# Loading w_in for the first two tiles in pieces of 384, 512 and 480 columns, each summed in a PSUM bank of its own

## The chip, the cores and the metric

The kernel runs on one core of a Trainium2 chip. A core has a matrix engine (TensorE, PE in the profile), a vector engine (VectorE, DVE), an activation engine (ScalarE, ACT), a general one (GpSimd, POOL) and a queue engine (SyncE, SP); 16 DMA engines move data between the chip's main memory and the core's SBUF. TensorE multiplies out of SBUF into PSUM, which has eight banks of 512 float32 columns over 128 partitions. The metric is the device time of one execution in microseconds; the median of the runs of a kernel is compared.

## What is computed

x is 2048 rows of 512 columns. Two blocks work on it and a gate mixes them. Block A is linear attention with 32 heads of 16 and learned softmax features. Block B, the one this change touches, is a gated MLP with spatial mixing: x is multiplied by w_in (512 by 1376), a GELU follows, the right half is normalised over its columns and mixed over the rows with w_sp, and the product of both halves goes through w_out.

```
def _B_ref(x, w_in, w_sp, b_sp, w_out):
    B, S, D = x.shape
    F = w_in.shape[-1]
    Fh = F // 2
    z = _gelu(jnp.einsum('bsd,df->bsf', x, w_in))
    z1 = z[..., :Fh].copy()
    z2 = _layernorm(z[..., Fh:], axis=-1)
    g = jnp.einsum('ts,bsf->btf', w_sp, z2) + b_sp[None, :, None]
    return jnp.einsum('bsf,fd->bsd', z1 * g, w_out)
...
g = _sigmoid((x * gate_w).sum(-1, keepdims=True))
a = _A_ref(x, A_wqkv, A_w_phi, A_wo)
b = _B_ref(x, B_w_in, B_w_sp, B_b_sp, B_w_out)
return g * a + (1 - g) * b
```

## The kernel before

The 2048 rows are 16 tiles t of 128. All input is bf16 and stays in SBUF. The order of instructions on each engine is written out by hand: what the program lists first for an engine runs first on it, and semaphores are put in where one engine's instruction reads or overwrites what another one, or a DMA, has written.

The work runs in three stages. In the first, about a quarter of the time, every tile's rows are multiplied with w_in into PSUM (`z_piece`), passed through GELU into the buffer `zz` on ACT (`z_gelu`, `z_post`) and their column statistics are taken on DVE; products for block A are threaded between. In the second, 32 half tiles of w_sp times zz (`gg_half`) run among block A's key features; in the third the rest of these run among block A's queries and the output products (`out_part`).

The inner dimension of 512 is four slices of 128 (dt). `xT` holds x transposed, slice by slice, as the stationary operand; `w_in` is the moving operand, with one column more than the reference's 1376: column F holds gate_w, so the gate's product falls out of the same matmuls. It is written by `gate_column` (L208), a small matmul that turns gate_w's four rows into a column, and a cast on DVE (L212).

The change is in the first microseconds:

- x for tiles 0 and 1 is loaded as rows into `xn` (L108 on SP's queue, L109 on ACT's), transposed on TensorE (`x_transpose`, L193) and copied to `xT` by DVE for tile 0 and by ACT for tile 1 (`x_copy`, L200), in three steps over the slices. The xT of all later tiles comes by transposing DMAs on SP (L123 for tiles 2 and 3, L129 for the rest).
- w_in is loaded with seven DMAs (L112, L122), called A to E here. A is columns 0 to 256 and B is 256 to 512, both with slices 0 and 1 on SP's queue and slices 2 and 3 on ACT's. C and D are columns 512 to 1024, slices 0 and 1 and then 2 and 3, both on SP. E is columns 1024 to 1376 of all slices, on SP. The fifth transfer of a queue is held until the first one has landed, the sixth until the second, and so on.
- ACT's queue then loads gate_w (`gw`, L120), and ACT loads its GELU table (L121).
- Until the first data are there, TensorE runs matmuls on constants (`spin`, L187), whose result nobody reads.
- Tiles 0 and 1 then go through w_in together, slice by slice: columns 0 to 256, 256 to 512 and 512 to 1024 of both, with ACT's gelu of tile 0 and `gate_column` behind the second piece; then the last piece (353 columns with the gate's) of tile 0, its gelu, gate and statistics (`z_post`), and the same of tile 1, whose gelu over all 1376 columns is one instruction. Every later tile takes three pieces of 512, 512 and 353 columns.
- A tile's sums lie in three banks, 0 to 2 for even tiles and 3 to 5 for odd ones (`zbank`, L67); columns n0 to n1 lie at n0 to n1 of these 1536 columns.

Of the kernel before, what the change touches and what calls it, by code (L numbers as in the profile page):

```python
# [7 lines left out]
AF = mybir.ActivationFunctionType  # L8
# [6 lines left out]
P = 128  # L15
# [4 lines left out]
F = 1376  # L20
# [3 lines left out]
NDT = D // P  # L24
CH = 512
# [14 lines left out]
def kernel(  # L40
# [14 lines left out]
    nc = tc.nc  # L55
# [11 lines left out]
    def zbank(t):  # L67
        b = 3 * (t % 2)
        return ps[:, b:b + 3, :].rearrange("p b n -> p (b n)")

    xT = pers.tile([P, NDT, S], BF16, name="xT")
    w_in = pers.tile([P, NDT, F + 1], BF16, name="w_in")
# [6 lines left out]
    zz = pers.tile([P, NT, F], BF16, name="zz")  # L79
# [15 lines left out]
    gth = st[:, 1, :]  # L95
# [7 lines left out]
        out=ident[:], in_=ident[:], pattern=[[-1, P]],  # L103
# [3 lines left out]
    w_in_v = B_w_in.rearrange("(dt p) f -> p dt f", p=P)  # L107
# [3 lines left out]
    def load_w_in(eng, d0, d1, n0, n1):  # L111
        eng.dma_start(out=w_in[:, d0:d1, n0:n1], in_=w_in_v[:, d0:d1, n0:n1])  # L112

    HC = CH // 2
    for n0 in (0, HC):
        load_w_in(nc.sync, 0, 2, n0, n0 + HC)
        load_w_in(nc.scalar, 2, 4, n0, n0 + HC)
    for d0 in (0, 2):
        load_w_in(nc.sync, d0, d0 + 2, CH, 2 * CH)
    nc.scalar.dma_start(out=gw[:], in_=gate_w.rearrange("(dt p) -> dt p", p=P))  # L120
    nc.scalar.activation(out=st[:, 9, 0:1], in_=ones[:, 0:1], func=AF.Gelu_apprx_tanh)  # L121
    nc.sync.dma_start(out=w_in[:, :, 2 * CH:F], in_=w_in_v[:, :, 2 * CH:F])  # L122
    nc.sync.dma_start_transpose(out=xT[:, :, 2 * P:CH], in_=x2[2 * P:CH, :])  # L123
    nc.sync.dma_start(
        out=wv[:, :, :],
        in_=A_wqkv[:, 2 * D:3 * D].rearrange("(dt p) n -> p dt n", p=P),
    )
    for q in range(1, NCH):
        nc.sync.dma_start_transpose(  # L129
            out=xT[:, :, q * CH:(q + 1) * CH], in_=x2[q * CH:(q + 1) * CH, :]  # L130
        )
        if q == 1:
            nc.sync.dma_start(
                out=wphiW[:, :, :],
                in_=A_w_phi.rearrange("(g h) e f -> (h e) g f", g=NDT),
# [3 lines left out]
        out=bcolb[:, :, :], in_=B_b_sp.rearrange("(t p) -> t p", p=P)  # L139
# [7 lines left out]
    for t in range(WSLOTS):  # L147
        load_wsp(t)
    nc.sync.dma_start(
        out=w_out[:, 0:NFT - 1, :],  # L150
        in_=B_w_out[0:(NFT - 1) * P, :].rearrange("(ft p) n -> p ft n", p=P),
# [4 lines left out]
        out=w_out[0:last_m, NFT - 1, :], in_=B_w_out[(NFT - 1) * P:FH, :]  # L156
    )
    nc.sync.dma_start(
        out=wo[:, :, :], in_=A_wo.rearrange("(g p) n -> p g n", p=P)
# [4 lines left out]
        out=mask16[:], in_=mask16[:], pattern=[[-16, 8]],  # L164
# [3 lines left out]
        out=mask16[:], in_=mask16[:], pattern=[[16, 8]],  # L168
# [8 lines left out]
    def z_piece(t, n0, n1, d0=0, d1=NDT):  # L177
        zb = zbank(t)
        for dt in range(d0, d1):
            nc.tensor.matmul(  # L180
                zb[:, n0:n1], lhsT=xT[:, dt, t * P:(t + 1) * P], rhs=w_in[:, dt, n0:n1],
                start=(dt == 0), stop=(dt == NDT - 1),
            )

    Z_PIECES = [(0, CH), (CH, 2 * CH), (2 * CH, F + 1)]

    def spin(n):  # L187
        for _ in range(n):
            nc.tensor.matmul(
                ps[:, 5, 0:P], lhsT=ones, rhs=ones, start=True, stop=True  # L190
            )
# [16 lines left out]
    def gate_column():  # L208
        nc.tensor.matmul(  # L209
            ps[:, 6, 0:NDT], lhsT=gw[:], rhs=ident[0:NDT, 0:NDT], start=True, stop=True  # L210
        )
        nc.vector.tensor_copy(out=w_in[:, :, F], in_=ps[:, 6, 0:NDT])  # L212

    def z_gelu(t, n0, n1):
        nc.scalar.activation(  # L215
            out=zz[:, t, n0:n1], in_=zbank(t)[:, n0:n1], func=AF.Gelu_apprx_tanh
        )

    def z_post(t, done=0):
        zb = zbank(t)  # L220
        z_gelu(t, done, F)
        nc.scalar.activation(out=gth[:, t:t + 1], in_=zb[:, F:F + 1], func=AF.Tanh, scale=0.5)
        for h in range(2):
            nc.vector.bn_stats(  # L224
                out=stats[:, t, h, :], in_=zz[:, t, FH + h * HF:FH + (h + 1) * HF]
            )
        nc.vector.bn_aggr(out=mv[:, t, :], in_=stats[:, t, :, :].rearrange("p h s -> p (h s)"))
# [63 lines left out]
    def build_wphi():  # L291
        nc.vector.tensor_tensor(
            out=wphi[:].rearrange("p g (h f) -> p g h f", h=8),
            in0=wphiW[:, :, None, :].to_broadcast([P, NDT, 8, DH]),
            in1=mask16[:, None, :, None].to_broadcast([P, NDT, 8, DH]),
            op=ALU.mult,
        )
# [178 lines left out]
        x_copy(0, d0, d1)  # L476
        x_copy(1, d0, d1)
    spin(4)
    for n0, n1 in ((0, HC), (HC, CH), Z_PIECES[1]):
        for dt in range(NDT):  # L480
            z_piece(0, n0, n1, dt, dt + 1)
            z_piece(1, n0, n1, dt, dt + 1)
        if n1 == CH:
            z_gelu(0, 0, CH)
            gate_column()
    z_gelu(0, *Z_PIECES[1])
    z_piece(0, *Z_PIECES[2])
    z_post(0, done=2 * CH)
    z_piece(1, *Z_PIECES[2])
    z_post(1)  # L490
    build_wphi()
    for t in range(2, NT):
        for n0, n1 in Z_PIECES:
            z_piece(t, n0, n1)
        z_post(t)
        if t >= VLAG:
            v_proj(t - VLAG)
        if 5 <= t < 13:
            fold(t - 5)
        if t in (3, 7, 11):  # L500
            ln_batch(t - 3, t + 1)
        if t == 14:
            ln_batch(12, 15)
        if t == 7:
            nc.vector.tensor_copy(out=bcol[:], in_=bcolb[:, 0, :])
        if t >= 5:
            z1_gate(t - 5)
# [81 lines left out]
```

## Time and profile before

| | us |
|---|---|
| median of 3 runs | 208.22 |
| lowest, highest | 207.81, 208.29 |
| the profiled execution, whole | 208.12 |
| its span, from the first to the last instruction | 206.4 |

| DMA queue | packets | MB |
|---|---|---|
| q1, what SP issues | 87360 | 23.87 |
| q10, what ACT issues | 3000 | 2.39 |

Times inside the profile count from the start of the span. PE, DVE, ACT and POOL are the engines above; PEld is TensorE's loading of the stationary operand, which runs beside its matmuls; SPq and ACTq are the queue instructions that issue a DMA. A matmul's shown duration includes the pipeline's end, so back-to-back matmuls overlap in it: the distance of their starts is what one costs. The granted clock of TensorE was 1.000 over the span. The page's chain that ended last gives PE 96%, DMA 2%. In it L405 (w_sp times zz) holds 36%, L180 (x times w_in) 18%, and the DMA of w_in 2%.

Two shares of the DMA view are of use for the first microseconds: the mean busy share of the 16 DMA engines and the GB/s that they moved. From 2.0 to 9.0 they moved 1.87 MB, 267 GB/s in the mean, of which q10 carried 0.39 MB. DMA issues that matter there, with KB each and the median time from issue to landing: w_in on SP, two of 256 KB (4.5 us), two of 128 KB (3.6), one of 352 KB (4.9); w_in on ACT, two of 128 KB (4.0); xn, 128 KB on each queue (2.5 on SP, 2.7 on ACT). These KB are of 1024 bytes.

### The profile page before, as it was taken

The numbers are of one execution on the slowest core, as the hardware profiler recorded it, in microseconds if no ns is written. First come the engines' busy times: TensorE is split into PE (matmuls) and PEld (weight loads), VectorE is DVE, ScalarE is ACT, GpSimd is POOL, SyncE is SP. The second block draws the span as 40 slices with busy tenths as digits, with TensorE's granted clock in tenths as the row PEclk, the third lists the DMA queues.
The fourth block names the chain that finished last, engine by engine and source line by source line (L and its number), as shares of the span: only waits on it lengthen the run. The fifth ranks groups of instructions, "written<-read, shape, count | busy, mean of one in ns | idle before, by whom it ended". The sixth has DMA issues, their size and how long they took to land.

```text
span 206.4 us, 3685 instructions
## 1 busy us (share of the span) xinstructions
PE 202.3 (98%) x1399; PEld 117.8 (57%) x1399; DVE 148.5 (72%) x304; ACT 82.1 (40%) x145; POOL 49.5 (24%) x46
## 2 busy tenths in 40 slices
PE   8999999999999999999999999999999999999994
PEld 8545555554455666666666667666455555555542
DVE  1049858385887888879898996798989788796500
ACT  4266767675684324250505102222524243341122
POOL 4000000000002353525352543032532252322000
PEclk9999999999999999999999999999999999999999
DMA  5999899997000638463757781145756974566451
GB/s 160 289 178 247 189 170 226 168 192 231 0 3 0 140 65 117 102 112 85 153 126 109 139 174 41 38 91 84 161 131 122 127 176 98 129 141 153 110 110 51
DMA packets 90378, 26.50 MB, mean 128 GB/s; under 512 B 84296, under 2 KB 90360, under 8 KB 90360
## 3 DMA queue, kind: packets, MB, share of 16 engines
q1 hardware_dynamic: 87360, 23.87, 60.2%
q10 hardware_dynamic: 3000, 2.39, 3.8%
q8 instruction: 11, 0.18, 0.4%
q14 instruction: 7, 0.06, 0.1%
HBM read 3.44 MB, written 2.10 MB: 27 GB/s over the span
## 4 chain that ended last, share of the span: by engine, by line
PE 96%; DMA 2%; SPq 0%; ACT 0%; issue 0%
PE ps L405 36%; PE ps L180 18%; PE ps L326 13%; PE ps L448 10%; PE ps L453 7%; PE ps L282 7%; DMA w_in<-in_B_w_in_dram 2%; PE ps L427 2%; PE ps L377 2%; PE ps L305 1%; SPq L112 0%; SPq L108 0%; ACT ob L457 0%; PE ps L209 0%
## 5 line engine op out<-in xcount | busy, mean ns | idle before, releaser
L405 PE MATMUL ps<-zz,wsp 128*128 128x344 bf16 x512 | 84.1, 309 | 0.0
L343 POOL TENSOR_TENSOR w_in<-w_in,rs 128x512 bf16<-128x512 bf16 x28 | 41.3, 1475 | 124.7 <-DVE rs L341 112.4
L405 PEld LDWEIGHTS <-wsp 128*128 128x128 bf16 x512 | 49.9, 98 | 28.1
L334 ACT ACTIVATE w_in<-ps 128x512 bf16<-128x512 f32 x56 | 30.1, 596 | 63.3 <-issue 21.4
L180 PE MATMUL ps<-w_in,xT 128*128 128x512 bf16 (+2 forms) x200 | 39.7, 350 | 0.4 <-DMA w_in<-in_B_w_in_dram 0.4
L339 DVE TENSOR_REDUCE zs<-w_in 128x64 f32<-128x1024 bf16 x28 | 33.8, 1209 | 0.0
L413 DVE SCALAR_TENSOR_TENSOR u<-ps,bcol,zz 128x344 bf16<-128x344 f32 x32 | 18.4, 574 | 18.6 <-PE ps L427 8.3
L180 PEld LDWEIGHTS <-xT 128*128 128x128 bf16 x200 | 19.1, 98 | 18.0 <-issue 0.8
L215 ACT ACTIVATE zz<-ps 128x1376 bf16<-128x1376 f32 (+2 forms) x18 | 21.4, 1190 | 18.6 <-PE ps L180 18.6
L448 PE MATMUL ps<-w_out,uT 128*128 128x512 bf16 (+2 forms) x102 | 23.5, 366 | 0.0
L224 DVE BATCH_NORM_STATS2 stats<-zz 128x6 f32<-128x344 bf16 x32 | 14.8, 505 | 11.1 <-ACT zz L215 11.1
L377 PE MATMUL ps<-vv,w_in 128*128 128x65 bf16 x128 | 21.7, 193 | 0.0
L343 DVE TENSOR_TENSOR w_in<-w_in,rs 128x512 bf16<-128x512 bf16 x28 | 19.4, 693 | 1.0
L341 DVE RECIPROCAL rs<-zs 128x64 f32<-128x64 f32 x32 | 17.7, 553 | 3.2
L457 ACT ACTIVATE ob<-ps 128x512 bf16<-128x512 f32 (+2 forms) x17 | 9.7, 572 | 25.1 <-PE ps L453 19.9
L453 PE MATMUL ps<-wo,oT 128*128 128x512 bf16 (+2 forms) x68 | 16.6, 366 | 0.0
L326 PEld LDWEIGHTS <-xT 128*128 128x128 bf16 x128 | 10.8, 98 | 9.9
L326 PE MATMUL ps<-wq,xT 128*128 128x512 bf16 x64 | 16.4, 379 | 0.0
L326 PE MATMUL ps<-wk,xT 128*128 128x512 bf16 x64 | 16.3, 379 | 0.0
L427 PE MATMUL ps<-kvx,wqkT 128*128 128x68 bf16 x128 | 15.8, 194 | 0.0
L282 PE MATMUL ps<-wv,xT 128*128 128x512 bf16 x64 | 15.6, 379 | 0.0
L448 PEld LDWEIGHTS <-uT 128*128 128x128 bf16 x102 | 9.5, 98 | 10.4
(56 smaller groups left out, 134.3 us busy)
## 6 DMA issues: line engine op xcount, KB each, us to landing
out_dram<-ob ACTq DMA_DIRECT2D x15, 128.0 KB, 2.1
w_out<-in_B_w_out_dram SPq DMA_DIRECT2D x1, 640.0 KB, 4.9
w_in<-in_B_w_in_dram SPq DMA_DIRECT2D x2, 256.0 KB, 4.5
wv<-in_A_wqkv_dram SPq DMA_DIRECT2D x1, 512.0 KB, 5.0
wo<-in_A_wo_dram SPq DMA_DIRECT2D x1, 512.0 KB, 5.3
w_in<-in_B_w_in_dram SPq DMA_DIRECT2D x1, 352.0 KB, 4.9
w_in<-in_B_w_in_dram ACTq DMA_DIRECT2D x2, 128.0 KB, 4.0
w_in<-in_B_w_in_dram SPq DMA_DIRECT2D x2, 128.0 KB, 3.6
```

What stands on the lines that cost most here:

```text
L180: nc.tensor.matmul(zb[:, n0:n1], lhsT=xT[:, dt, t * P:(t + 1) * P], rhs=w_in[:, dt, n0:n1], start=(dt == 0), stop=(dt == NDT - 1),)
L215: nc.scalar.activation(out=zz[:, t, n0:n1], in_=zbank(t)[:, n0:n1], func=AF.Gelu_apprx_tanh)
L282: nc.tensor.matmul(ps[:, b, :], lhsT=xT[:, dt, t * P:(t + 1) * P], rhs=wv[:, dt, :], start=(dt == 0), stop=(dt == NDT - 1),)
L326: nc.tensor.matmul(ps[:, b, :], lhsT=xT[:, dt, t * P:(t + 1) * P], rhs=w[:, dt, :], start=(dt == 0), stop=(dt == NDT - 1),)
L334: nc.scalar.activation(out=e[:, :, a, :], in_=src, func=AF.Exp, scale=sc)
L339: nc.vector.tensor_reduce(out=zs[:], in_=ev, axis=AX.X, op=ALU.add)
L343: eng.tensor_tensor(out=ev[:, sl, :], in0=ev[:, sl, :], in1=rs[:, sl, None].to_broadcast([P, H, DH]), op=ALU.mult,)
L377: nc.tensor.matmul(slots[:, g, 0:HW + 1], lhsT=ek_t[t][:, g, :, :].rearrange("p a n -> p (a n)"), rhs=vv[:, t, g, 0:HW + 1], start=(t == 0 ...
L405: nc.tensor.matmul(ps[:, b, 0:HF], lhsT=wsp[:, tt % WSLOTS, s, :], rhs=zz[:, s, FH + h * HF:FH + (h + 1) * HF], start=(s == 0), stop=(s == ...
L427: nc.tensor.matmul(slots[:, g, 0:QW], lhsT=eT_t[t][:, g, :], rhs=kvx[:, g, :], start=True, stop=True)
L448: nc.tensor.matmul(ps[:, b, n0:n1], lhsT=uT[:, ft, :], rhs=w_out[:, ft, n0:n1], start=(ft == 0), stop=False,)
L453: nc.tensor.matmul(ps[:, b, n0:n1], lhsT=oT[:, g, :], rhs=wo[:, g, n0:n1], start=False, stop=(g == NDT - 1),)
```

## The change

For the first two tiles the columns of w_in are cut at 384 and 896 rather than at 256, 512 and 1024 (`FIRST`). The pieces, called A', B' and E' here, have 384, 512 and 480 columns (481 with the gate's). A' and B' are each loaded half by SP and half by ACT, E' by SP alone and ahead of ACT's load of gate_w. Each piece's sums start at the first column of a bank of its own (`z_first`), so the gelus of tiles 0 and 1 read three banks in three instructions per tile (`z_gelu_first`), and the gate's sum of these tiles lies at column 480 of the third bank. Tile 1's gelus come behind its last matmuls in the program's order. `gate_column` stands behind the third slice of B'. Later tiles keep their pieces; what they read of w_in is the same.

```
--- before.py
+++ after.py
@@ -111,15 +111,13 @@
     def load_w_in(eng, d0, d1, n0, n1):
         eng.dma_start(out=w_in[:, d0:d1, n0:n1], in_=w_in_v[:, d0:d1, n0:n1])
 
-    HC = CH // 2
-    for n0 in (0, HC):
-        load_w_in(nc.sync, 0, 2, n0, n0 + HC)
-        load_w_in(nc.scalar, 2, 4, n0, n0 + HC)
-    for d0 in (0, 2):
-        load_w_in(nc.sync, d0, d0 + 2, CH, 2 * CH)
+    FIRST = [(0, 384), (384, 896), (896, F + 1)]
+    for n0, n1 in FIRST[0:2]:
+        load_w_in(nc.sync, 0, 2, n0, n1)
+        load_w_in(nc.scalar, 2, 4, n0, n1)
+    load_w_in(nc.sync, 0, NDT, FIRST[2][0], F)
     nc.scalar.dma_start(out=gw[:], in_=gate_w.rearrange("(dt p) -> dt p", p=P))
     nc.scalar.activation(out=st[:, 9, 0:1], in_=ones[:, 0:1], func=AF.Gelu_apprx_tanh)
-    nc.sync.dma_start(out=w_in[:, :, 2 * CH:F], in_=w_in_v[:, :, 2 * CH:F])
     nc.sync.dma_start_transpose(out=xT[:, :, 2 * P:CH], in_=x2[2 * P:CH, :])
     nc.sync.dma_start(
         out=wv[:, :, :],
@@ -216,10 +214,31 @@
             out=zz[:, t, n0:n1], in_=zbank(t)[:, n0:n1], func=AF.Gelu_apprx_tanh
         )
 
-    def z_post(t, done=0):
-        zb = zbank(t)
-        z_gelu(t, done, F)
-        nc.scalar.activation(out=gth[:, t:t + 1], in_=zb[:, F:F + 1], func=AF.Tanh, scale=0.5)
+    def z_first(t, k, dt):
+        n0, n1 = FIRST[k]
+        nc.tensor.matmul(
+            zbank(t)[:, k * CH:k * CH + n1 - n0], lhsT=xT[:, dt, t * P:(t + 1) * P],
+            rhs=w_in[:, dt, n0:n1], start=(dt == 0), stop=(dt == NDT - 1),
+        )
+
+    def z_gelu_first(t, k):
+        n0, n1 = FIRST[k]
+        n1 = min(n1, F)
+        nc.scalar.activation(
+            out=zz[:, t, n0:n1], in_=zbank(t)[:, k * CH:k * CH + n1 - n0],
+            func=AF.Gelu_apprx_tanh,
+        )
+
+    def z_post(t, first=False):
+        if first:
+            z_gelu_first(t, 2)
+            c = 2 * CH + F - FIRST[2][0]
+        else:
+            z_gelu(t, 0, F)
+            c = F
+        nc.scalar.activation(
+            out=gth[:, t:t + 1], in_=zbank(t)[:, c:c + 1], func=AF.Tanh, scale=0.5
+        )
         for h in range(2):
             nc.vector.bn_stats(
                 out=stats[:, t, h, :], in_=zz[:, t, FH + h * HF:FH + (h + 1) * HF]
@@ -476,18 +495,20 @@
         x_copy(0, d0, d1)
         x_copy(1, d0, d1)
     spin(4)
-    for n0, n1 in ((0, HC), (HC, CH), Z_PIECES[1]):
+    for k in range(2):
         for dt in range(NDT):
-            z_piece(0, n0, n1, dt, dt + 1)
-            z_piece(1, n0, n1, dt, dt + 1)
-        if n1 == CH:
-            z_gelu(0, 0, CH)
-            gate_column()
-    z_gelu(0, *Z_PIECES[1])
-    z_piece(0, *Z_PIECES[2])
-    z_post(0, done=2 * CH)
-    z_piece(1, *Z_PIECES[2])
-    z_post(1)
+            z_first(0, k, dt)
+            z_first(1, k, dt)
+            if k == 1 and dt == 2:
+                gate_column()
+        z_gelu_first(0, k)
+    for t in (0, 1):
+        for dt in range(NDT):
+            z_first(t, 2, dt)
+        if t == 1:
+            z_gelu_first(1, 0)
+            z_gelu_first(1, 1)
+        z_post(t, first=True)
     build_wphi()
     for t in range(2, NT):
         for n0, n1 in Z_PIECES:
```

## The prediction

> **What bounds the kernel now.** I read the profile from the whole to the place: first the page (busy shares, slices, the chain that ended last), then the chain and the timeline of the first 13 us, then the DMA views of that stretch. The page first:
>
> ```profile
> PE 202.3 (98%) x1399; PEld 117.8 (57%) x1399; DVE 148.5 (72%) x304; ACT 82.1 (40%) x145; POOL 49.5 (24%) x46
> ...
> PE   8999999999999999999999999999999999999994
> ...
> PEclk9999999999999999999999999999999999999999
> ```
>
> TensorE is busy 98% of a span of 206.4 us at full granted clock, and only the first slice is short of nine tenths. Behind that slice the chain of waits is PE matmul after PE matmul, so an edit of the first two tiles is worth what it moves the start of tile 2 on PE; everything later moves with it, one for one. The chain up to there:
>
> ```profile
> 1.25 0.42 SPq L112
> 1.67 0.05 issue
> 1.72 4.46 DMA w_in<-in_B_w_in_dram
> 6.18 0.04 issue
> 6.22 1.05 PE ps L180 x8
> 7.28 0.10 PE ps L209
> ```
>
> Columns are start, duration, what. PE waits for the second w_in piece that SP issued at 1.72 and that landed at 6.18. The timeline of PE shows what this costs:
>
> ```profile
> 4.64 1.15 PE L180 MATMUL ps<-w_in,xT 128*128 128x256 bf16 x8
> 6.22 1.05 PE L180 MATMUL ps<-w_in,xT 128*128 128x256 bf16 x8 [0.43 <-DMA w_in<-in_B_w_in_dram]
> 7.21 0.17 PE L209 MATMUL ps<-ident,gw 4*128 4x4 bf16 x1
> ```
>
> and two rows of the whole timeline show the last piece: the gate cast runs only when that piece is there (8.96), and PE's first 353-column matmul starts at 9.19, right behind it:
>
> ```profile
> 8.96 0.18 DVE L212 CAST w_in<-ps 128x4 bf16<-128x4 f32 x1 [4.12 <-DMA w_in<-in_B_w_in_dram]
> ...
> 9.19 0.46 PE L180 MATMUL ps<-w_in,xT 128*128 128x353 bf16 x2
> ```
>
> **Matmul prices.** In the chain four 512-column matmuls of L282 take 0.86, so 0.215 each. A steady tile of L180 (eight of 512, four of 353) takes 2.33, so a 353 takes (2.33 - 1.72)/4 = 0.1525. In a straight line between these, 384 columns cost 0.165 and 481 cost 0.203. The 256s start 0.11 apart. Tile 2 thus starts at 9.19 + 8 x 0.1525 = 10.41; its gelu at 12.93 agrees (10.41 + 2.33 and a pipeline's end of 0.19). Between 4.64 and 10.41 PE has 16 x 0.11 + 8 x 0.215 + 8 x 0.1525 = 4.70 of work and 0.10 of gate matmul; the remaining 0.97 is waiting: about 0.59 before 6.22, 0.11 inside the second piece, 0.16 before 9.19, and rounding. **That 0.97 (0.47% of the time) is all the change can win.**
>
> **When w_in lands.** Each issue's landing is its start plus the time that the trace gives to landing, as here for the last piece:
>
> ```profile
> L122 SPq DMA_DIRECT2D w_in<-in_B_w_in_dram x1: 469/469/469, 4.0 to 4.0; - x1
> ...
> DMA to landing us min/median/max: 4.9/4.9/4.9
> ```
>
> So: xn about 3.4; piece A (columns 0 to 256) SP half 1.25 + 2.8 = 4.05, ACT half 1.24 + 3.1 = 4.34; B SP half 6.18, ACT half 1.7 + 4.9 = 6.6; C and D (512 to 1024, SP alone) 2.22 + 4.8 = 7.02 and 3.54 + 4.3 = 7.84; E (the last 352) 3.96 + 4.9 = 8.86. What moved meanwhile, by windows (the last two columns are DMA share and GB/s):
>
> ```profile
> 3.00:3.60 0.60, 0.60 (x9) 0.50 (x7) 0.00 (x0) 0.60 (x1) 0.00 (x0) 1.00 1.12 335
> 3.60:5.00 1.40, 1.40 (x15) 1.29 (x14) 0.82 (x3) 1.35 (x5) 0.00 (x0) 1.00 0.90 220
> 5.00:6.00 1.00, 0.79 (x8) 0.54 (x6) 0.00 (x0) 0.17 (x1) 0.00 (x0) 1.00 0.94 293
> 6.00:7.00 1.00, 0.78 (x7) 0.67 (x7) 0.00 (x0) 0.00 (x0) 0.00 (x0) 1.00 1.06 342
> ```
>
> With 268 kB before 3.0, these give 469 kB at 3.6, 777 at 5.0, 1070 at 6.0 and 1412 at 7.0; xn and w_in are 262 + 1409 = 1671 kB, reached at about 7.85. E landed 1.0 behind that, A's later half 0.5 behind its own 524 kB (3.85). The engines are 90% to 112% busy throughout: no place in a queue kept E waiting, the bytes did. There is a slow spell, 3.6 to 5.0.
>
> **The change part by part.**
> *Transfers.* Seven w_in issues (five on SP, two on ACT) become five: A' 393 kB, B' 524, E' 492, the same 1409 kB. SP issues its three by 2.7, since the fifth transfer of a queue waits for its first (SP waited 0.8 for xn before D). E' is thus given out 1.7 earlier (3.96 before), behind the same bytes in its queue. Hidden by the queue: worth nothing unless the pace changes. The pace of the forecast: the spell at 220 stays where it is in time; behind it 342 (the rate with one queue on long rows) instead of 293 gives 5.0 + (1671 - 777)/342 = 7.61, and E' lands 1.0 later at 8.62. If nothing in the pace changes it is 8.86. I take the middle, **8.74**, since the 293 stands beside the tail of B's ACT half, which B' has too. Ends: 340 from 3.6 on, 8.1 with the lag of 1.0 and 7.6 with A's lag of 0.5; 220 for as long as both queues carry pieces, 9.27 (below).
> *First two pieces.* A' is 655 kB of the sum with xn, at 4.45; the halves land at about 4.65 (SP, 0.3 ahead as for A) and 4.95. Eight matmuls of 0.165 from 4.66 end at 5.98, with the ACT half wanted at 5.32. B' is at 5.0 + (1179 - 777)/342 = 6.18; with 1.0 of lag the ACT half lands at 7.2, the SP half by B's distance earlier at 6.75. Eight of 0.215 from 6.75 end at 8.47 (ACT half wanted at 7.61), with the gate matmul at 8.57. So the last piece, not B', decides; B' has 0.5 in hand.
> *Last piece.* It grows from 353 to 481 columns a matmul, 8 x 0.203 = 1.62 against 1.22, and all of it lies behind the last landing. Landing to first matmul was 9.19 - 8.86 = 0.33 (wait, cast, wait) and stays. Tile 2 starts at 8.74 + 0.33 + 1.62 = 10.69 against 10.41: **+0.28**.
> *Fewer matmuls.* 24 for 32, 4.66 against 4.70 of work; the 0.04 is inside the sum above and alone worth nothing, as PE waits in between.
> *ACT.* Tile 1 has three gelus (0.49, 0.60 and 0.57 in a line through 0.46 for 352 and 0.60 for 512) for one of 1.32: 0.34 more. Tile 0's last gelu starts near 10.05, so tile 1's tanh ends near 12.6; cover is tile 2's gelu, not ready before 10.69 + 2.33 + 0.19 = 13.2. Without that cover it would cost up to 0.34. Tile 3 writes the banks of tile 1 from 13.0 on, its third bank 1.7 later: free by then. The statistics on DVE come 0.4 later; DVE's next work there is wphi at 15.31.
> *Gate matmul.* It moves behind the third step of B', still 0.10 on PE; gw had landed by 7.21, before any place it now has. The cast waits for E' as it waited for E; behind it on DVE stand only the statistics.
> *What SP does next.* The transposes of x for tiles 2 and 3 are issued at 3.54 for 4.47, with 1.95 of issue; wv follows at 5.5 (needs A'), the next transpose waits for B' near 6.75 (7.08 before), wphi and wqkT keep their places to within 0.4. Cover: tile 2's xT landed at 4.47 + 5.4 = 9.87, 1.0 behind E; now about 9.75, needed at 10.69.
>
> **Sum.** The profiled execution took 208.12 for its span of 206.4, the rest lying around it. 208.12 + 0.28 = 208.40; the median of the runs shown is 0.10 above the profiled one, so **208.5**.
>
> **Rivals.**
> 1. *Same pace to the byte.* Row width buys nothing. The DMA view from 3.0 to 3.4, nearly all 512-byte rows, and from 6.4 to 7.0, rows of 1024 and 704 bytes:
>
> ```profile
> DMA packets 273, 0.14 MB, mean 343 GB/s; under 512 B 13, under 2 KB 273, under 8 KB 273
> ```
>
> ```profile
> DMA packets 263, 0.21 MB, mean 348 GB/s; under 512 B 8, under 2 KB 263, under 8 KB 263
> ```
>
> Then E' lands at 8.86: +0.41, 208.6. Against: 293 in the mixed stretch. The Trainium skill (DMA: Bandwidth & Descriptors, Specifications) says that rows from 512 bytes up already go at line rate, which speaks against any gain of this change; the two windows agree, and by that rule alone the time would be this rival's.
> 2. *The slow spell follows the two queues* (slower). For: 220 GB/s came while A and B of both queues interleaved and 342 came with SP alone. Against: 335 from 3.0 to 3.6 with both. Now both carry pieces until 1179 kB: 3.6 + 710/220 = 6.83; E' another 492/342 = 1.44, and 1.0 of lag: 9.27. Tile 2 at 9.27 + 0.33 + 1.62 = 11.22: +0.81, 209.0. It decides from a landing of E' after 9.08 on (0.62 over before).
> 3. *The spell came of the many short transfers and goes* (faster). For: it sits where A ends and B and C begin. 340 from 3.6: B' at 5.7, E' at 7.15; with A's lag of 0.5, B' starts at 6.0 and E' lands at 7.64: tile 2 at 9.6, -0.8, 207.4. With a lag of 1.0 it is 10.05, -0.36, which counts as no change. Against: the lag was 1.0 from C on.
>
> **How the numbers follow.** A measurement of this kernel tells some 0.3%, 0.62 us, from no change. Forecast 0.31 (208.5), same pace 0.18 (208.6), slow spell 0.30 (209.0), spell gone 0.21 (207.4). Faster 0.21, same 0.49, slower 0.30. E' landing at 8.2 to 9.0 gives the likeliest its own range of 208.0 to 208.8; with the others the range is 207.4 to 209.3, the upper end a little over rival 2, for a lag longer than 1.0.
>
> **What would show it.** The cast of the gate column starts 0.1 behind the landing of E': near 8.85 by the forecast, after 9.2 by rival 2, before 8.0 by rival 3. PE's first 481-column matmul follows 0.24 later and tile 2 starts 1.62 behind that. The first eight matmuls start near 4.66, B' near 6.75, each with one DMA wait before it. I am wrong in kind if tile 2's start and the end of the span move by different amounts, if ACT or xT holds tile 2, or if B' ends after E' has landed.

## The result and the profile after

| | median us | lowest, highest | runs |
|---|---|---|---|
| before | 208.29 | 207.81, 208.47 | 11 |
| changed | 208.74 | 207.85, 209.80 | 11 |

The changed kernel takes 1.0034 times as long as the one before (95% interval 1.0018 to 1.0050); in a second comparison it was 1.0041 (1.0026 to 1.0056). By these ratios it is slower by some 0.7 to 0.85 us, about at the bound of 0.3% that the prediction set; the medians stand 0.45 apart in the first comparison and 0.93 in the second. Its runs scatter over 2 us where those before scatter over 0.7. The profiled execution is the slowest of the changed runs, 209.80 with a span of 208.1, so it shows the mechanism at its largest; a second one, of 208.79, is below.

The page after has lost TensorE's second slice:

```profile
PE 201.9 (97%) x1391; PEld 116.8 (56%) x1391; DVE 148.6 (71%) x304; ACT 82.1 (39%) x147; POOL 49.2 (24%) x46
...
PE   8599999999999999999999999999999999999994
```

The chain of waits (start, duration, what) names the same transfer as before, the second piece that SP issued at 1.72:

```profile
1.72 6.60 DMA w_in<-in_B_w_in_dram
8.32 0.04 issue
8.36 1.46 PE ps L219 x6
9.82 0.11 PE ps L207
9.92 2.21 PE ps L219 x10
```

It was 4.46 there and is 6.60 now. On PE the eight matmuls of A' start on time, and then nothing runs for over two microseconds:

```profile
4.67 1.46 PE L219 MATMUL ps<-w_in,xT 128*128 128x384 bf16 x8
8.36 1.46 PE L219 MATMUL ps<-w_in,xT 128*128 128x512 bf16 x6 [2.23 <-DMA w_in<-in_B_w_in_dram]
9.75 0.17 PE L207 MATMUL ps<-ident,gw 4*128 4x4 bf16 x1
9.86 2.28 PE L219 MATMUL ps<-w_in,xT 128*128 128x512 bf16 x10
11.97 1.25 PE L178 MATMUL ps<-w_in,xT 128*128 128x512 bf16 x5
```

Tile 2 starts at 11.97 (10.39 before). From there on the two kernels' matmuls keep the same distances to within 0.001 us up to the last one, so the 1.58 here is nearly all of the 1.68 that the execution lost; behind the last matmul 3.18 pass to the end of the span, 3.02 before. The last piece was no better off: the gate cast ran at 10.12, right behind E' (landed 2.22 + 7.8 = 10.0):

```profile
10.12 0.18 DVE L210 CAST w_in<-ps 128x4 bf16<-128x4 f32 x1 [5.20 <-DMA w_in<-in_B_w_in_dram]
```

In the windows (DMA share and GB/s are the last two columns) the reader is to see that the rate was not what failed:

```profile
3.60:5.00 1.40, 1.28 (x15) 1.06 (x14) 0.82 (x3) 1.39 (x5) 0.00 (x0) 1.00 1.02 259
5.00:6.00 1.00, 1.00 (x7) 0.57 (x6) 0.00 (x0) 0.07 (x1) 0.00 (x0) 1.00 0.94 300
6.00:7.00 1.00, 0.13 (x1) 0.00 (x0) 0.00 (x0) 0.49 (x1) 0.00 (x0) 1.00 1.00 322
...
8.40:9.00 0.60, 0.60 (x3) 0.25 (x3) 0.00 (x0) 0.00 (x0) 0.00 (x0) 1.00 0.46 61
9.00:10.00 1.00, 1.00 (x6) 0.40 (x5) 0.00 (x0) 0.00 (x0) 0.00 (x0) 1.00 0.39 70
```

The slow spell is milder than before (259 for 220). Over the windows from 2.0 to 7.0 both kernels moved the same 1.40 to 1.41 MB. Then from 8.4 to 10.0 next to nothing moves while E' is still awaited. Who is late shows in the marks that a transfer leaves in the trace as it lands. Each plain transfer of 128 rows leaves 16 of them, gate_w with its four rows four late ones. The Trainium skill (DMA: Bandwidth & Descriptors, on why a DMA increments its semaphore by 16) says that each of the DMA engines taking part counts once when its share has landed, and that only the full count means that all is there; the sixteen and the four agree. So the first and the last mark are the fastest and the slowest engine (us):

```
                    B or B', SP    B or B', ACT    E or E'        tile 2 starts
before              4.55  6.18     4.93  6.63      8.81  8.88     10.39
changed             5.43  8.32     5.89  8.83      9.88 10.00     11.97
changed, again      5.15  7.37     5.93  8.00      8.70  8.85     10.97
before, again       4.63  5.65     4.91  5.95      8.57  8.63     10.14
```

In the changed profile 15 engines had delivered SP's half of B' by 7.20 and one came at 8.32. In its packets that engine then takes one packet of each queue in turn, at the ordinary 46 ns, until it is through; it had lost its time before, where single packets at the start of B' took up to 1.17 us.

### The profile page after: what moved, and what is told of

The parts are those of the page before. It is cut to its first block, busy times and chain, and to the rows that moved or that the text cites. A ratio compares the mean times of both kernels' runs of the same rounds, so it can differ in the third digit from the quotient of the medians.

```text
span 208.1 us, 3668 instructions
## 1 busy us (share of the span) xinstructions
PE 201.9 (97%) x1391; PEld 116.8 (56%) x1391; DVE 148.6 (71%) x304; ACT 82.1 (39%) x147; POOL 49.2 (24%) x46
## 4 chain that ended last, share of the span: by engine, by line
PE 95%; DMA 3%; SPq 0%; ACT 0%; issue 0%
PE ps L424 36%; PE ps L178 16%; PE ps L345 13%; PE ps L467 10%; PE ps L472 7%; PE ps L301 7%; DMA w_in<-in_B_w_in_dram 3%; PE ps L446 2%; PE ps L396 2%; PE ps L219 2%; PE ps L324 1%; SPq L112 0%; SPq L108 0%; ACT ob L476 0%; PE ps L207 0%
## 5 line engine op out<-in xcount | busy, mean ns | idle before, releaser
L178 PE MATMUL ps<-w_in,xT 128*128 128x512 bf16 (+1 forms) x168 | 34.4, 357 | 0.0
L178 PEld LDWEIGHTS <-xT 128*128 128x128 bf16 x168 | 16.0, 97 | 15.8
L213 ACT ACTIVATE zz<-ps 128x1376 bf16<-128x1376 f32 x14 | 18.5, 1318 | 15.1 <-PE ps L178 15.1
L345 PEld LDWEIGHTS <-xT 128*128 128x128 bf16 x128 | 10.8, 98 | 9.9
```

What stands on the lines that cost most here:

```text
L178: nc.tensor.matmul(zb[:, n0:n1], lhsT=xT[:, dt, t * P:(t + 1) * P], rhs=w_in[:, dt, n0:n1], start=(dt == 0), stop=(dt == NDT - 1),)
L213: nc.scalar.activation(out=zz[:, t, n0:n1], in_=zbank(t)[:, n0:n1], func=AF.Gelu_apprx_tanh)
L345: nc.tensor.matmul(ps[:, b, :], lhsT=xT[:, dt, t * P:(t + 1) * P], rhs=w[:, dt, :], start=(dt == 0), stop=(dt == NDT - 1),)
```

## The experiments

The theories behind the expectations: the loss is a fixed cost of the longer last piece; or it is the landing of the engine that falls behind, and then the question is what makes it fall behind. All edits are to the changed kernel where nothing else is said. Medians stand with the ratio to the kernel before that was run beside them.

**The changed kernel again.**

> The changed kernel itself, for a second profile beside the one of the result. Landing theory (the time is set by the last landing of E', which varies from run to run because single DMA engines fall behind): E' lands anywhere from 8.6 to 10.0, the span is that landing + 0.33 + 1.62 + 195.9 to within 0.2, and the runs scatter over 1 us or more. Fixed-cost theory (the change costs a fixed amount, 0.4 for the longer last piece, and the landing is that of before): E' lands at 8.8 to 9.0 and the runs scatter no more than those of the kernel before, some 0.6.

208.86, ratio 1.0041 (1.0026 to 1.0056), six runs from 208.18 to 209.22. PE in its profile:

```profile
4.79 1.71 PE L219 MATMUL ps<-w_in,xT 128*128 128x384 bf16 x8
7.41 1.46 PE L219 MATMUL ps<-w_in,xT 128*128 128x512 bf16 x6 [0.90 <-DMA w_in<-in_B_w_in_dram]
8.80 0.17 PE L207 MATMUL ps<-ident,gw 4*128 4x4 bf16 x1
8.90 2.24 PE L219 MATMUL ps<-w_in,xT 128*128 128x512 bf16 x10
10.97 2.19 PE L178 MATMUL ps<-w_in,xT 128*128 128x512 bf16 x10
```

E' had landed by 8.85 and the gate cast was done by 9.18, and yet the last piece starts at 9.35, where B' ends: 7.41 + 1.72, and 0.20 for the gate matmul with the gap of 0.10 ahead of it. ACT's half, landed at 8.00, held nothing, since its first matmul came at 8.27. So in this execution B' decided, not E'. The scatter is that of the landing theory, but the landing that counts is B' more often than E': of the eight profiles with these cuts, the one with a single queue included, the last piece started right behind B' in five and behind E' in one, and in the other two both ended within 0.05 of each other.

**A plain transfer between E' and the transposing one.**

```diff
     load_w_in(nc.sync, 0, NDT, FIRST[2][0], F)
...
+    wv_v = A_wqkv[:, 2 * D:3 * D].rearrange("(dt p) n -> p dt n", p=P)
+    nc.sync.dma_start(out=wv[:, 0:1, :], in_=wv_v[:, 0:1, :])
     nc.sync.dma_start_transpose(out=xT[:, :, 2 * P:CH], in_=x2[2 * P:CH, :])
-    nc.sync.dma_start(
-        out=wv[:, :, :],
-        in_=A_wqkv[:, 2 * D:3 * D].rearrange("(dt p) n -> p dt n", p=P),
-    )
+    nc.sync.dma_start(out=wv[:, 1:NDT, :], in_=wv_v[:, 1:NDT, :])
```

> The first slice of wv (131 kB, a plain transfer) is issued between E' and the transpose of x for tiles 2 and 3. Barrier theory (the transposing DMA right behind E' holds back the landing of E' on all engines until the last one is through): the first and the last of the 16 engines' counts of E' lie 1 us or more apart, as those of B' do, rather than within 0.1, and E' lands some 0.4 earlier, time 208.3. Lag theory (only the engine that is furthest behind matters): E' lands where it did, spread or not, time as the changed kernel's.

E' now landed from 7.33 to 9.14, spread over 1.81 where it had been 0.15 or less, and the slice of wv, now next to the transposing transfer, took over the bunching (9.42 to 9.52). The barrier is there: the transfer right ahead of the transposing one, E' before and the slice of wv now, lands on all engines at once, behind the slowest. It costs little, for the slowest engine's 9.14 is late by itself: 208.57, ratio 1.0032 (1.0017 to 1.0046).

**The transposing transfer later.**

```diff
-    nc.sync.dma_start_transpose(out=xT[:, :, 2 * P:CH], in_=x2[2 * P:CH, :])
     nc.sync.dma_start(
         out=wv[:, :, :],
         in_=A_wqkv[:, 2 * D:3 * D].rearrange("(dt p) n -> p dt n", p=P),
     )
+    nc.sync.dma_start(
+        out=wphiW[:, :, :],
+        in_=A_w_phi.rearrange("(g h) e f -> (h e) g f", g=NDT),
+    )
+    nc.sync.dma_start_transpose(out=xT[:, :, 2 * P:CH], in_=x2[2 * P:CH, :])
...
```

> All of wv and of w_phi go ahead of that transpose, so that it is issued near 5.3 rather than 3.6 and its data come behind 0.54 MB more. If its issue beside B' makes engines fall behind: the spread of B' over the 16 engines falls from 2.9 to 1.2 or less and E' lands by 8.5. If not: B' is spread by 1.6 to 2.9 as before and E' lands at 8.8 to 10. In both the transposed tiles come late, near 11.5, so tile 2 waits some 1 us for them and the time is no measure of E'.

SP's half of B' landed from 5.10 to 7.93, spread 2.83, and E' was whole at 9.60. The early issue of the transpose, from 5.05 on here, is not what delays the engine. The time of 209.72 has two parts: tile 2 started at 12.13, right behind xT (12.09), where the late E' alone would have let it start at 11.58.

**No gate_w load.**

```diff
-    nc.scalar.dma_start(out=gw[:], in_=gate_w.rearrange("(dt p) -> dt p", p=P))
+    nc.gpsimd.memset(gw[:], 0.0)
```

> The load of gate_w, four rows of 256 bytes on four engines behind B' on ACT's queue, is left out; GpSimd writes zeros in its place, so the gate is one half everywhere. If that little transfer is what makes engines late: B' and E' spread less, E' lands by 8.6 and the time falls by 0.4 or more to 208.3. If not: as the changed kernel, 208.7.

This kernel leaves out the gate's weights, and with one transfer fewer SP issues the transpose at 2.74. It took 208.75, ratio 1.0042 (1.0027 to 1.0057); SP's half of B' was spread by 2.05 and whole at 7.21. The load of gate_w is not the cause.

**SP silent until E', or until A', has landed.**

```diff
+    hold = pers.tile([P, 8], BF16, name="hold")
+    nc.sync.dma_start(out=hold[0:1, :], in_=w_in[0:1, 0, 896:904])
     nc.sync.dma_start_transpose(out=xT[:, :, 2 * P:CH], in_=x2[2 * P:CH, :])
```

The second kernel copies from `w_in[0:1, 2, 0:8]`.

> Ahead of the transpose of x for tiles 2 and 3 a copy of 16 bytes out of E' is put in SP's queue, which waits for E' to have landed; so SP issues nothing from 2.7 to that landing. Issue theory (an engine's packets on SP's queue stall while SP's next transfers are being generated, from 3.6 on): the stalls at the start of B' vanish, B' spreads by 0.6 over the 16 engines like A', and E' lands by 7.9, its counts spread. Boundary theory (packets stall where one transfer ends and the next begins, whatever SP does): B' still spreads by 1.6 or more and E' lands at 8.4 to 9.6. In both the transposed tiles come 3 to 4 us late and the time is 210 to 212.

> The same with a copy out of ACT's half of A': SP issues its next transfer near 7 (4.9 and the 2 of the small copy if the transpose waits for nothing else, from 4.9 on). Issue theory: B' begins undisturbed, its spread is below 1.2 and E' lands by 8.3; the time 208.0 to 208.4 if the transposed tiles are in time. Boundary theory: as the changed kernel, 208.7.

In the first, SP issued nothing between 2.79 and 8.93:

```profile
1.27 1.52 SPq L112 DMA_DIRECT2D w_in<-in_B_w_in_dram  x3
8.93 0.80 SPq L122 DMA_DIRECT2D hold<-w_in  x1
9.77 1.34 SPq L123 DMA_TRANSPOSE xT<-in_A_x_dram  x1
```

and still B' was spread by 1.58 on SP's half and 2.09 on ACT's, and E' was whole at 8.85. This time ACT's queue had reached B' first, and the long packets (up to 0.56) were on that queue. The issue theory falls by this profile. The time of 211.83 is the late transpose. In the second the small copy went out at 4.96 and the transpose at 5.81, earlier than I had put it; SP's half of B' was spread by 1.82 and whole at 7.22, and the time was 208.60, ratio 1.0033 (1.0016 to 1.0049): as the changed kernel.

**The cuts at 512 and 1024.** Two sizes change, and not one as the expectation says: the last piece is the 353 columns of the kernel before, and the first piece grows from 384 to 512.

```diff
-    FIRST = [(0, 384), (384, 896), (896, F + 1)]
+    FIRST = [(0, 512), (512, 1024), (1024, F + 1)]
```

> The change with the cuts at 512 and 1024 (three pieces of 512, 512 and 353 columns), one size changed: the last piece is as long as that of the kernel before. If the longer last piece is what the change costs: 208.3. If the landings are: A' lands near 5.2, B' 0.4 later than in the changed kernel and B' decides: tile 2 starts 1.72 + 0.10 + 1.22 behind B' near 7.9, time 208.7 to 209.2.

208.21, ratio 1.0012 (1.0000 to 1.0025). The PE rows of its profile:

```profile
5.00 3.40 PE L219 MATMUL ps<-w_in,xT 128*128 128x512 bf16 x14 [0.22 <-DVE xT L202]
8.33 0.17 PE L207 MATMUL ps<-ident,gw 4*128 4x4 bf16 x1
8.44 1.81 PE L219 MATMUL ps<-w_in,xT 128*128 128x512 bf16 x10
10.09 3.14 PE L178 MATMUL ps<-w_in,xT 128*128 128x512 bf16 x15
```

PE starts 0.2 to 0.3 later and then hardly stops; from 8.88 the last piece takes 1.20, where the changed kernel's takes 1.63 (9.35 to 10.97). B' was whole at 7.16 and E' at 8.10, and the longer first piece gives PE work until 6.7. So the landings moved as well, and this run does not tell the shorter last piece from them; its profiled execution took 207.92, 0.29 less than the median. Once more, to see whether that early landing was luck:

> The kernel with cuts at 512 and 1024 once more, for a second profile and more runs. Longer-last-piece theory: 208.0 to 208.3, E' landing where it may; if its early landing of 8.10 was the point, it lands by 8.3 again; if it was luck, 8.6 to 9.0, with the time up by as much.

208.37, ratio 1.0014 (1.0005 to 1.0023), E' whole at 8.49, tile 2 at 10.21:

```profile
4.97 3.56 PE L219 MATMUL ps<-w_in,xT 128*128 128x512 bf16 x14
8.46 0.17 PE L207 MATMUL ps<-ident,gw 4*128 4x4 bf16 x1
8.57 1.81 PE L219 MATMUL ps<-w_in,xT 128*128 128x512 bf16 x10
```

Neither of the two cases: E' came 0.39 later than in the profile above and tile 2 0.13 later. No landing decided here. SP's half of B' was there at 6.64, but PE was busy with A' until 7.07, because the first two distances of its matmuls were 0.38 and 0.42 where 0.22 is usual, and from 4.97 on it never waited.

**The kernel before, again.**

> The kernel before, for a second profile of it. Lag theory (the landings vary with the engine that falls behind, in the changed kernel more): E lands between 8.4 and 9.2 and its second piece B is spread over the 16 engines by 1.3 to 2.0, time 207.8 to 208.4. If the landings of the kernel before are much steadier or earlier than 8.86, the changed order of the transfers costs more than the longer last piece does.

207.92 beside 208.00; SP's half of B was spread by 1.02, less than I had put, E landed at 8.63, and tile 2 started at 10.14. So E landed at 8.63 and 8.88 before, and E' at 8.85 and 10.00 in the two profiles of the changed kernel. The second piece is earlier and steadier before: whole at 5.95 and 6.63, for 8.00 and 8.83.

**The longer last piece alone, in the kernel before.** Cut in loads and matmuls moved from 1024 to 896.

```diff
+    C2 = 896
     for d0 in (0, 2):
-        load_w_in(nc.sync, d0, d0 + 2, CH, 2 * CH)
+        load_w_in(nc.sync, d0, d0 + 2, CH, C2)
...
-    nc.sync.dma_start(out=w_in[:, :, 2 * CH:F], in_=w_in_v[:, :, 2 * CH:F])
+    nc.sync.dma_start(out=w_in[:, :, C2:F], in_=w_in_v[:, :, C2:F])
...
-    z_piece(0, *Z_PIECES[2])
...
+    z_piece(0, C2, F + 1, p0=2 * CH)
```

> The kernel before with one part of the change alone: the cut at 1024 moves to 896 in loads and matmuls (C and D lose 128 columns, E gains them, the last piece has 481 columns and a bank of its own). Longer-last-piece theory: all of w_in is as late as before, the work behind it grows by 8 x 0.051 = 0.41, time 0.3 to 0.5 over the kernel before. Transfer theory (the loss comes of the order and the number of the transfers): within 0.15 of the kernel before.

208.85, ratio 1.0047 (1.0035 to 1.0060): more than expected.

```profile
4.89 2.21 PE L182 MATMUL ps<-w_in,xT 128*128 128x256 bf16 x16
7.03 0.17 PE L211 MATMUL ps<-ident,gw 4*128 4x4 bf16 x1
7.13 1.48 PE L182 MATMUL ps<-w_in,xT 128*128 128x384 bf16 x8
9.49 3.82 PE L182 MATMUL ps<-w_in,xT 128*128 128x481 bf16 x18 [0.88 <-DVE w_in L214]
```

The pieces ahead are done near 8.4 and PE stands until E is there (9.18). Tile 2 starts at 11.11, 0.72 later than in the first profile before: 0.41 of longer work (predicted so) and 0.30 of later landing. The work that is missing ahead of E cost nothing by itself: in both profiles before, too, the last piece started 0.31 behind the landing of E (8.88 and 8.63), so E at 9.18 would have cost as much there. What is late is E's own slowest engine: single packets of E took up to 1.01 between 5.8 and 7.6, for at most 0.06 and 0.62 before. Whether a longer E makes that likelier one profile can't tell; but all six runs (208.81 to 209.28) lost more than the 0.41.

**Half way: cuts at 448 and 960.**

```diff
-    FIRST = [(0, 384), (384, 896), (896, F + 1)]
+    FIRST = [(0, 448), (448, 960), (960, F + 1)]
```

> The change with the cuts at 448 and 960 (448, 512 and 417 columns), between the changed kernel and the one with 512. Longer-last-piece theory: the work behind the last landing is 8 x 0.178 = 1.42, 0.20 less than the changed kernel's and 0.20 more than with 512: half way between these two, 208.4. If the first piece's earlier start counts instead (PE starts 0.25 earlier than with 512): at or below the 512 kernel, 207.9 to 208.1.

208.39, ratio 1.0011 (1.0002 to 1.0020), level with the cut at 512. The median is the 208.4 of the first theory, but the cut at 512, run beside it, gave 208.37 and 1.0014: there is no step between 417 and 353 columns, where the price of the matmuls puts 0.20. That leaves 481 columns as the step too far; the profiled execution, the fastest of its twelve at 207.77, has tile 2 at 9.94.

**All of w_in on one queue.**

```diff
-        load_w_in(nc.sync, 0, 2, n0, n1)
-        load_w_in(nc.scalar, 2, 4, n0, n1)
+        load_w_in(nc.sync, 0, NDT, n0, n1)
```

> The changed kernel with A' and B' each as one transfer of all four slices on SP's queue; ACT's queue carries xn and gate_w alone. Two-queue theory (an engine falls behind because its two queues' transfers end and begin against each other; in every profile so far the queue that reached B' first had the long packets): B' is spread by 1.0 or less over the 16 engines, no packet of B' takes over 0.2, E' lands by 8.3 and B' is whole by 6.9, so tile 2 starts near 10.3 and the time is 208.1 to 208.3. Place theory (the second piece's start near 4.3 is slow for another reason, whatever the queues): B' is spread by 1.5 or more, whole at 7.2 or later, time 208.6 to 209. A' is wanted whole 0.7 later for its first two slices, so PE may start up to 0.2 later in both.

209.49, ratio 1.0066 (1.0047 to 1.0085), slower than either case. The profiled execution took 208.62, less than most of its runs:

```profile
5.21 1.95 PE L218 MATMUL ps<-w_in,xT 128*128 128x384 bf16 x8 [0.17 <-DMA w_in<-in_B_w_in_dram]
7.36 1.46 PE L218 MATMUL ps<-w_in,xT 128*128 128x512 bf16 x6 [0.19 <-DMA w_in<-in_B_w_in_dram]
...
10.92 2.35 PE L177 MATMUL ps<-w_in,xT 128*128 128x512 bf16 x11
```

B' is spread by 1.48 and whole at 7.31, and four of its packets, between 4.3 and 5.4, take 0.36 to 0.77. By then ACT's queue had nothing left to carry, so there was nothing to interleave, and the two-queue theory falls as well by this profile. One thing more differs here: the transposing transfer is issued from 2.82 on, for 3.59 in the changed kernel. The waits in the traces show why: the two queues share eight semaphores, so it is the ninth transfer of both together that is held until the first has landed, and not the fifth of one queue, as it was put ahead of the prediction. Why this order is the slowest of all in the runs without a profile stays open.

## Why the prediction held, and where it did not

The time came out at 208.74 for a forecast of 208.5 in a range of 207.4 to 209.3. The movement, 0.34%, lies just across the bound of 0.3% between "same" and "slower", with its interval on both sides.

- **One for one.** Held but for a tenth: span minus start of tile 2 was 195.97 to 196.13 in all profiles but the one where the transpose was held until E' had landed. The difference lies behind the last matmul. From there to the end it is 3.02 to 3.04 in the kernel before, with the longer last piece alone and with one queue, and 3.10 to 3.18 in the ten others. These 0.06 to 0.16 us are in no term of the prediction, and why they come is open.
- **Matmul prices.** 8 x 0.203 = 1.62 for the last piece was measured as 1.63 (10.35 to 11.97 and 9.35 to 10.97), 1.22 for 353 columns as 1.20. The gate matmul was put at 0.10 and takes 0.20, with a gap of 0.10 ahead of it that is in every profile; so 0.10 of the 0.97 that the prediction called waiting was not to be won.
- **First piece.** PE started at 4.60 to 4.95 with these cuts and two queues, for a forecast of 4.66. In five of the eight profiles with these cuts some of the first matmuls then stood 0.32 apart, for 0.16 in the others, at a granted clock of 1.00. It cost nothing there, since B' came later still.
- **The last piece's landing.** Forecast 8.74; measured 8.85 in the typical execution, 8.67 with gate_w left out, and 10.0 in the slowest. The cast ran 0.12 behind it there (10.12).
- **The step that failed: "the last piece, not B', decides; B' has 0.5 in hand".** SP's half of B' was put at 6.75, from a lag of 1.0 that I took to be the same for every piece. It landed at 7.37 in the typical profile, between 6.95 and 7.93 in the experiments with these cuts and two queues, and at 8.32 in the slowest. PE started B' at 7.41 rather than 6.75, and B' and E' behind it are 1.72 + 0.20 + 1.63 of work with nothing left to cover a wait: tile 2 at 10.97 for a forecast of 10.69. The prediction had named this as a sign of being wrong in kind, that B' ends after E' has landed: it does in seven of the eight profiles with these cuts (9.35 after 8.85 in the typical one). I had worked with the mean rate and a fixed lag; what lands a piece is its slowest engine, and B' of 256 KB a queue was spread by 1.4 to 2.9 in the profiles with these cuts and two queues, for 1.0 to 1.7 with the 128 KB of B before. The size alone does not do it: with the cuts at 448 and 512 B' has the same 256 KB a queue and was spread by 0.8 to 1.4, though these three profiles show executions 0.3 to 0.6 faster than their kernels' medians.
- **The cost of 0.28 was too small by up to about half a microsecond**: the ratios give 0.7 to 0.85 us. In the typical profile tile 2 starts 0.28 later than forecast because B' decides, and 0.06 to 0.16 lies behind the last matmul. How much of the loss is the longer last piece is not shown. Two kernels that end on 481 columns, the changed one and the one before with that change alone, lose 0.34 to 0.47%; those that end on 417 or 353 lose 0.11 to 0.14%. But the first piece and the landings change with the cuts, 417 columns cost no more than 353, and 481 columns alone lost more than the whole change.
- **That the time came so near is in part luck.** The forecast of 208.5 is 0.24 below the median, with a path that E' decides; the path was B', and the landing of E' that the sum rests on was right without deciding.
- **Rival 2, the slow spell following the two queues, is not what happened**, though its time of 209.0 is as near as the forecast's: the rate was 259, 300 and 322 GB/s where it should have stayed at 220. Rival 3 was wrong in the rate, which was 259 and not 340 behind 3.6, and so in the landing of E'. Rival 1 had E' right (8.86) for the usual execution and B' wrong with the forecast.
- **Covers.** ACT's longer gelus, the moved gate matmul and the transposed tiles cost nothing: the transposed rows landed at 10.94, 1.0 before tile 2 took them, and every matmul behind tile 2 kept its place.

What stays open is why single packets take 0.2 to 1.3 us near the start of the second piece. By one to three profiles each, it is not the issue of later transfers, the load of gate_w, or the two queues. The loading of ACT's table at 2.93 to 4.21 and the copies of xT on DVE and ACT at 4.1 to 5.3 lie nearby in time, and neither was taken away; but they stand at the same times in the first profile with the cut at 512, where no packet of w_in behind 3.5 took over 0.1, so alone they do not make such packets.

## What to carry to other kernels

While a kernel still waits for its first data, price each piece by the work that lies behind its last landing: 128 columns more in the last piece were 0.41 us of matmuls with nothing left to hide them. Take the landing of a piece from its slowest DMA engine and from more than one execution, since mean rates of 259 to 322 GB/s hid an engine that was a microsecond or more behind. Compare the profiled execution with the median before reading it as typical: those here lay from 1.06 above their kernel's median to 0.87 below. Fewer and larger transfers saved nothing here: none of the three sets of cuts was faster than the kernel before.

## What the runs showed of the hardware that was not expected

**A transposing transfer can hold up the landing of the plain one ahead of it.** The 16 marks of E and E' come within 0.06 to 0.15 in the ten profiles that have the transposing transfer right behind, though 480 of the 512 packets of E' had ended 1.1 earlier than the last in the slowest execution (8.40 and 9.51). In the four profiles with another transfer between, the same E' was spread over 1.26 to 2.19; with the plain slice of wv there, the slice landed within 0.10. It does not hold for every pair: w_phi, in rows of 32 bytes, landed over 0.48 to 2.03 in thirteen profiles with a transposing transfer right behind it. Meanwhile the transposing transfer's first 256-byte packets stay open for up to 2.5 us behind E' (changed kernel, from 7.36 on).

**Packets have a price of their own.** The usual duration of one in the trace, by its bytes:

```
512 B 27 ns   704 B 34 ns   768 B 36 ns   960 B 44 ns   1024 B 46 ns
```

That is some 8 ns and 0.037 ns a byte, or 19 GB/s an engine at 512 bytes and 22 at 1024. The Trainium skill (DMA: Bandwidth & Descriptors, Specifications) puts line rate at 512 bytes and more; by these durations 512 is 15% short of 1024, which the windows of the prediction (343 and 348 GB/s) did not show and which gained the change no time.
